# Scores of two slots in one TensorE burst, and PSUM banks shared to make room for it

## The chip, the cores and the metric

The kernel runs on one core of a Trainium2 chip. The time is that of the whole kernel on the device, in microseconds (us): inputs come from HBM, the result goes back to HBM. The engines of the core are TensorE (PE: matrix products, results go to PSUM, which has eight banks of 512 floats per partition), VectorE (DVE), ScalarE (ACT), GpSimd (POOL) and SyncE (SP, which here only issues DMAs).

## The reference

Attention with a threshold, then a two-layer network with a gated activation:

```python
def _attn_ref(q, k, v, tau):                    # 8 batches, 8 heads, 576 tokens, 64 per head
    scale = 1.0 / np.sqrt(q.shape[-1])
    scores = scale * np.matmul(q, k.transpose(0, 1, 3, 2))
    thresh = np.max(scores, axis=-1, keepdims=True) - tau
    scores = np.where(scores >= thresh, scores, -1000000000.0)
    scores = scores - np.max(scores, axis=-1, keepdims=True)
    attn = np.exp(scores)
    attn = attn / (np.sum(attn, axis=-1, keepdims=True) + 1e-09)
    return np.matmul(attn, v)

def _moe_ref(x, w_in, w_out):                   # 4608 tokens, 512 -> 2048 -> 512
    h = x @ w_in
    relu6 = np.clip(h + 3.0, 0.0, 6.0)
    g = h * relu6 / 6.0
    return g @ w_out
```

Inputs and the result are float32. Between the two parts, the heads of a token are put side by side.

## The kernel before

Four heads of a batch are a "quad", two heads a "pair": 16 quads. A quad is cut into nine "slots": slots 0 to 3 and 4 to 7 are four blocks of 128 queries of each pair, and slot 8 holds the 64 queries that are left of both pairs (576 = 4 x 128 + 64). One slot is 128 query rows of two heads, `a` = 0 and 1, which stand on the two halves of TensorE's rows. There are 144 slots, `n` = 0 to 143, in one loop, in which every engine's work stands in the order of the program.

The parts that matter here (cuts are marked):

```python
    ps_s = ctx.enter_context(tc.psum_pool(name="ps_s", bufs=2))   # scores: 2 x 2 banks
    ps_h = ctx.enter_context(tc.psum_pool(name="ps_h", bufs=1))   # projection: 2 banks
    ps_o = ctx.enter_context(tc.psum_pool(name="ps_o", bufs=1))   # output tile: 1 bank
    ps_m = ctx.enter_context(tc.psum_pool(name="ps_m", bufs=1))   # small products: 1 bank
    # ... cut
    def scores(quad, slot):
        tiles = [ps_s.tile([P, 2, 512], F32, tag="s", name="s") for _ in range(2)]
        for hf in range(2):                       # two halves of 288 keys
            if slot < 8:
                pair, t = 2 * quad + slot // 4, slot % 4
                for a in range(2):
                    nc.tensor.matmul(tiles[a][:, hf, 0:HALF], qT_of(pair)[a * 64:(a + 1) * 64, t * P:(t + 1) * P],
                                     keys(pair, a, hf), start=True, stop=True)
            # ... cut: slot 8, two pairs of 64 queries each
        return tiles

    def sm_max(sl):                               # scores out of PSUM, with the maximum of each row
        # ... cut
        for i, ps in enumerate(sl.tiles):
            nc.vector.tensor_scalar(out=sl.s[:, i, :].rearrange("p (a b) -> p a b", a=2), in0=ps[:, :, 0:HALF],
                                    scalar1=1.0, scalar2=None, op0=Alu.mult, op1=Alu.max,
                                    accum_out=sl.m[:, i:i + 1])
        nc.gpsimd.tensor_scalar(out=sl.bias[:], in0=sl.m[:], scalar1=-scale, scalar2=tau, op0=Alu.mult, op1=Alu.add)

    def mm1(item, pool=None):                     # projection: 256 or 320 tokens x 256 hidden units
        b, ni, c0, w = item
        hps = (pool or ps_h).tile([P, 2, 512], F32, tag="s" if pool else "h", name="h")
        for n in range(2):
            for ki in range(KI):
                nc.tensor.matmul(hps[:, n, 0:w], w_in_sb[:, ki, (ni + n) * P:(ni + n + 1) * P],
                                 xT[b][:, ki, c0:c0 + w], start=(ki == 0), stop=(ki == KI - 1))
        return hps[:, :, 0:w]
    # ... cut: mm1_relu on ScalarE or VectorE, mm1_gate on VectorE (into gbuf),
    #          mm2_part: 4 of the 16 matmuls of an output tile, mm2_out: the tile out of PSUM

    for n, sl in enumerate(queue):
        # ... cut
        if prev is not None:
            for i in range(2):
                sm_exp(prev, i)                   # ScalarE
        if n + 1 < len(queue):
            sm_max(queue[n + 1])                  # VectorE

        if slot != 8 and todo1:
            item, then = todo1.pop(0)
            h = mm1(item)
            r = mm1_relu(h, on_act=(slot in ((0, 1, 3, 4, 5) if quad >= 2 * NB else (0, 2, 3, 4))))
            mm1_gate(item, h, r)
            todo2.extend(then)
        # ... cut: transposes on TensorE in the first slots
        if prev is not None:
            sm_recip(prev)                        # VectorE
        pieces = 0 if slot == 3 else 1            # output pieces: one per slot, two in slot 0 or 1
        # ... cut: mm2_part for each piece
        for i in range(2):
            sm_mask(sl, i)                        # ScalarE
        if n == 1 or slot == 0 and quad > 0:
            evict = transpose_q(2 * quad + 1)     # on VectorE from batch 2 on
        elif n == 2 or slot == 1:
            evict = transpose_k(2 * quad + 1)
        elif slot == 3 and quad > 0:
            av_main(2 * quad - 1)                 # attention times v, and its copy out by VectorE
        elif slot == 4 and quad > 0:
            av_rest(quad - 1)
        # ... cut: slots 4, 5 and 6 transpose for the next quad, slot 8: av_main(2 * quad)
        if n + 2 < len(queue):
            queue[n + 2].tiles = scores(queue[n + 2].quad, queue[n + 2].slot)
        if prev is not None:
            sm_norm(prev)                         # GpSimd, then a transposing DMA
```

After the loop stand the rest of the projections and output tiles, which take turns in three PSUM buffers.

Of the kernel before, what the change touches and what calls it, by code (L numbers as in the profile page):

```python
# [16 lines left out]
HALF = 288  # L17
# [4 lines left out]
def kernel(  # L22
# [21 lines left out]
    N2 = 28  # L44
    scale = 1.0 / math.sqrt(D)
# [15 lines left out]
    ps_s = ctx.enter_context(tc.psum_pool(name="ps_s", bufs=2))  # L61
    ps_h = ctx.enter_context(tc.psum_pool(name="ps_h", bufs=1))
    ps_o = ctx.enter_context(tc.psum_pool(name="ps_o", bufs=1))
    ps_m = ctx.enter_context(tc.psum_pool(name="ps_m", bufs=1))

    ctx.enter_context(tc.manual_schedule())

# [5 lines left out]
    xT = {}  # L73
    loads = []
# [103 lines left out]
    def warm_up(count):  # L178
        warm = ps_h.tile([P, 2, 512], F32, tag="h", name="warm")
        for _ in range(count):  # L180
            nc.tensor.transpose(warm[:, 0, 0:P], identf[:], identf[:])
# [26 lines left out]
    def bank(name):  # L208
        nonlocal turn
        turn += 1  # L210
        if now < N2 and turn % 2:
            return ps_o.tile([P, 512], F32, tag="o", name=name)
        return ps_m.tile([P, 512], F32, tag="m", name=name)
# [12 lines left out]
    def main_pe(src, pair):  # L226
        ps = bank("tp")
        n = pair % 2
        for t in range(4):
            nc.tensor.transpose(ps[:, t * P:(t + 1) * P], src[:, t, 2 * n:2 * n + 2, :], identf[:])  # L230
        return ps

    def transpose_q(pair):
        nq = nat[pair // 2][0]
        if by_pe(pair):
            ps = main_pe(nq[:, 0:1024].rearrange("p (t h d) -> p t h d", h=4, t=4), pair)
            return lambda: nc.vector.tensor_copy(out=qT_of(pair)[:, 0:512], in_=ps[:])
        n = pair % 2
        nc.vector.transpose(out=qT_of(pair), in_=nq[:, n * S:(n + 1) * S])

    def transpose_k(pair):
# [5 lines left out]
        ps = main_pe(nat[pair // 2][1], pair)  # L247
        return lambda: copy_out(kT_of(pair)[:, 64:576], ps[:])

    def transpose_rest(quad, of_k=True, of_q=True):  # L250
        ps = bank("tr")
        nq, _, kr = nat[quad]
        of_q = of_q and by_pe(2 * quad)
        if of_k:
            nc.tensor.transpose(ps[:, 0:P], kr[:], identf[:])
        if of_q:
            nc.tensor.transpose(ps[:, P:2 * P], nq[:, 1024:1152], identf[:])

        def evict():
            qT, kT = qkT[quad]  # L260
            both = ps[:].rearrange("p (w n t) -> p w n t", n=2, t=64)
# [7 lines left out]
    def keys(pair, a, hf):  # L269
        kT = kT_of(pair)  # L270
        c0 = 64 * (1 - a) + hf * HALF
        return kT[a * 64:(a + 1) * 64, c0:c0 + HALF]


    def scores(quad, slot):
        tiles = [ps_s.tile([P, 2, 512], F32, tag="s", name="s") for _ in range(2)]
        for hf in range(2):
            if slot < 8:
                pair, t = 2 * quad + slot // 4, slot % 4
                for a in range(2):  # L280
                    nc.tensor.matmul(tiles[a][:, hf, 0:HALF], qT_of(pair)[a * 64:(a + 1) * 64, t * P:(t + 1) * P],  # L281
                                     keys(pair, a, hf), start=True, stop=True)
            else:
                for n in range(2):
                    for a in range(2):
                        pair = 2 * quad + n
                        nc.tensor.matmul(tiles[a][n * 64:(n + 1) * 64, hf, 0:HALF],  # L287
                                         qT_of(pair)[a * 64:(a + 1) * 64, 512:S], keys(pair, a, hf),
                                         start=True, stop=True)
        return tiles  # L290
# [4 lines left out]
    def sm_max(sl):  # L295
# [5 lines left out]
        for i, ps in enumerate(sl.tiles):  # L301
            nc.vector.tensor_scalar(out=sl.s[:, i, :].rearrange("p (a b) -> p a b", a=2), in0=ps[:, :, 0:HALF],  # L302
# [30 lines left out]
    def pe_transpose(sl):  # L333
        ps = ps_h.tile([P, 2, 1024], BF16, tag="h", name="pt")
        ps = ps[:].rearrange("p a b -> p (a b)")[:, 0:2 * S].rearrange("p (c t) -> p c t", t=P)
        pn = sl.pn[:].rearrange("p a b -> p (a b)")
        for c in range(9):
            nc.tensor.transpose(ps[:, c, :], pn[:, c * P:(c + 1) * P], identb[:])
        return lambda: nc.vector.tensor_copy(out=sl.dst, in_=ps)


    def av(ps, pair, pT, cols):
        b, hp = divmod(pair, NPAIR)
        vm, vr = vsb[b]
        for c in range(4):
            for a in range(2):
                nc.tensor.matmul(ps[a * 64:(a + 1) * 64, :], vm[:, 2 * hp + a, c * D:(c + 1) * D],  # L347
                                 pT[:, 5 * a + c, cols], start=(c == 0), stop=False)
        for a in range(2):
            nc.tensor.matmul(ps[a * 64:(a + 1) * 64, :], vr[:, a, hp, :], pT[:, 4, cols], start=False, stop=True)  # L350

    def av_main(pair):
        b, hp = divmod(pair, NPAIR)
        if hp == 0:
            xT[b] = x_pool.tile([P, KI, S], BF16, tag="xT", name="xT")
        ps = bank("av")
        av(ps[:], pair, pts[pair], slice(0, 512))
        o0 = 64 if b % 2 else 0
        nc.vector.tensor_copy(out=xT[b][:, hp, o0:o0 + 512], in_=ps[:])  # L359

    def av_rest(quad):
        b, g = divmod(quad, 2)
        ps = bank("ar")
        for n in range(2):
            av(ps[:, n * 64:(n + 1) * 64], 2 * quad + n, ptr[quad], slice(n * 64, (n + 1) * 64))
        o0 = 0 if b % 2 else 512
        nc.vector.tensor_copy(out=xT[b][:, 2 * g:2 * g + 2, o0:o0 + 64],
                              in_=ps[:, 0:P].rearrange("p (a b) -> p a b", a=2))
# [273 lines left out]
```

## Time and profile before

| | |
|---|---|
| time, median of 3 runs | 546.87 us (545.75 to 548.74) |
| span of the profiled execution | 543.9 us |
| PE busy | 524.2 us, 96% |
| ACT busy | 459.9 us, 85% |
| DVE busy | 432.6 us, 80% |
| POOL busy | 278.3 us, 51% |
| granted TensorE clock | 0.998 |
| last scores of the loop begin, end of the span | 482.1, 543.9 us |

A profile line of a group reads: line of the kernel, engine, operation, what it writes and reads, shape, count, then busy time and mean ns of one, then the engine's idle time just before and what ended it. A timeline line reads: start and duration in us, engine, line, operation, tiles, form, count. A list of waits gives us in total, times, longest. "PEld" is TensorE's loading of weights; `x8` for one slot's scores means four float32 products of two passes each.

### The profile page before, as it was taken

What the parts mean: (1) busy time and instruction counts of PE and PEld (TensorE: products, weight loads), DVE (VectorE), ACT (ScalarE), POOL (GpSimd) and SP (SyncE); (2) the same over time, 40 slices, a digit from 0 to 9 for tenths busy, and PEclk for the clock granted to TensorE, in tenths of its full rate; (3) what the DMA queues carried; (4) which work ended last, traced back from release to release, by engine and by line L of the source; (5) the groups of instructions that cost most, each with busy time, mean ns of one, the idle gap of its engine ahead of it and who ended that gap; (6) DMA issues with size and microseconds to landing.
All of it is one profiled execution on the core that took longest, in us unless ns stands there. A gap on an engine that the chain in (4) does not pass through costs nothing.

```text
span 543.9 us, 11450 instructions
## 1 busy us (share of the span) xinstructions
PE 524.2 (96%) x3801; PEld 300.9 (55%) x3801; DVE 432.6 (80%) x1059; ACT 459.9 (85%) x985; POOL 278.3 (51%) x502
## 2 busy tenths in 40 slices
PE   8999899999999999899999999999999999999997
PEld 6665565545545555555555555545555555554663
DVE  3789888888978788888989788888989788974540
ACT  3999989978989899897989899997989899993440
POOL 1787879555455445654456445654456444451000
PEclk9999999999999999999999999999999999999999
DMA  5899999969989898998689798998689886544102
GB/s 125 128 156 158 143 148 179 181 83 177 158 159 182 136 167 149 155 176 146 112 152 201 130 168 132 183 159 145 133 149 202 134 163 111 111 102 104 40 17 81
DMA packets 308139, 76.63 MB, mean 141 GB/s; under 512 B 291056, under 2 KB 303600, under 8 KB 308080
## 3 DMA queue, kind: packets, MB, share of 16 engines
q1 hardware_dynamic: 289472, 66.59, 69.6%
q0 software_dynamic: 17408, 8.92, 14.3%
q8 instruction: 30, 0.49, 0.4%
q10 hardware_dynamic: 1200, 0.39, 0.3%
q14 instruction: 29, 0.24, 0.1%
HBM read 36.70 MB, written 9.44 MB: 85 GB/s over the span
## 4 chain that ended last, share of the span: by engine, by line
PE 60%; ACT 11%; DVE 11%; issue 3%; DMA 2%; POOL 2%; DVEq 0%; POOLq 0%
PE h L377 18%; PE o L406 17%; PE s L281 16%; ACT s L309 4%; PE av L347 4%; ACT s L314 4%; DVE s L302 4%; ACT r L386 2%; DVE g L394 2%; DMA pR<-pn 2%; DVE r L388 2%; PE s L287 1%; POOL pn L322 1%; DVE osb L414 1%; PE av L350 1%
## 5 line engine op out<-in xcount | busy, mean ns | idle before, releaser
L322 POOL TENSOR_SCALAR pn<-s,rinv 128x576 bf16<-128x576 f32 x288 | 211.7, 748 | 122.9 <-issue 49.7
L302 DVE TENSOR_SCALAR_CACHE_REDUCE s<-s 128x576 f32<-128x576 f32 x288 | 205.8, 752 | 32.5 <-PE s L281 20.9
L309 ACT ACTIVATE s<-s,bias 128x576 f32<-128x576 f32 x288 | 205.9, 763 | 6.3 <-POOL bias L305 5.9
L314 ACT ACTIVATE s<-s 128x576 f32<-128x576 f32 x288 | 192.5, 670 | 0.3
L281 PE MATMUL s<-kT,qT 64*128 64x288 f32 x1024 | 169.8, 429 | 2.1 <-DVE s L302 1.3
L377 PE MATMUL h<-xT,w_in_sb 128*128 128x320 bf16 (+1 forms) x1024 | 144.8, 287 | 4.2 <-DVE g L394 3.1
L406 PE MATMUL o<-w_out_sb,g 128*128 128x512 bf16 x576 | 140.7, 379 | 2.8 <-DVE osb L414 2.8
L281 PEld LDWEIGHTS s<-kT,qT 64*128 64x128 f32 x1024 | 96.2, 186 | 60.2 <-DVE s L302 24.8
L377 PEld LDWEIGHTS <-w_in_sb 128*128 128x128 bf16 x1024 | 91.4, 98 | 68.2 <-issue 33.1
L394 DVE SCALAR_TENSOR_TENSOR g<-r,h 128x512 bf16<-128x512 f32 (+1 forms) x128 | 96.4, 755 | 30.2 <-ACT r L386 28.7
L386 ACT ACTIVATE r<-h,three 128x640 f32<-128x640 f32 (+1 forms) x85 | 62.8, 740 | 42.5 <-PE h L377 41.0
L406 PEld LDWEIGHTS <-g 128*128 128x128 bf16 x576 | 55.6, 98 | 56.4 <-issue 7.7
L305 POOL TENSOR_SCALAR bias<-m 128x2 f32<-128x2 f32 x144 | 27.3, 190 | 89.2 <-DVE s L302 71.4
L314 ACT ACTIVATION_READ_ACCUMULATOR s<-s 128x1 f32 x288 | 54.4, 189 | 0.0
L414 DVE TENSOR_SCALAR osb<-o 128x512 f32<-128x512 f32 x31 | 21.0, 676 | 22.1 <-PE o L406 21.9
L347 PE MATMUL av<-pT,vm 128*64 128x512 bf16 x256 | 33.7, 385 | 1.7 <-DMA pT<-pn 1.3
L388 DVE TENSOR_SCALAR r<-h 128x512 f32<-128x512 f32 (+1 forms) x43 | 32.4, 753 | 0.0
L347 PEld LDWEIGHTS <-vm 128*64 128x64 bf16 x512 | 17.7, 110 | 25.2 <-issue 15.8
L359 DVE CAST xT<-av 128x512 bf16<-128x512 f32 x32 | 21.9, 684 | 10.9 <-PE av L350 10.8
L317 DVE RECIPROCAL rinv<-rsum 128x2 f32<-128x2 f32 x144 | 22.9, 159 | 2.3 <-ACT s L314 2.3
L302 DVE DVE_READ_ACCUMULATOR s<-s 128x1 f32 x288 | 24.0, 83 | 0.0
L287 PE MATMUL s<-kT,qT 64*64 64x288 f32 x256 | 21.5, 416 | 0.6 <-DVE s L302 0.6
(57 smaller groups left out, 226.2 us busy)
## 6 DMA issues: line engine op xcount, KB each, us to landing
out_dram<-osb SPq DMA_DIRECT2D x31, 256.0 KB, 2.6
nq<-in_q_dram SPq DMA_DIRECT2D x96, 72.0 KB, 2.9
km<-in_k_dram SPq DMA_DIRECT2D x96, 64.0 KB, 2.6
vm<-in_v_dram POOLq DMA_DIRECT2D x16, 256.0 KB, 6.1
km<-in_k_dram SPq DMA_DIRECT2D x16, 128.0 KB, 3.9
w_in_sb<-in_moe_w_in_dram POOLq DMA_DIRECT2D x16, 128.0 KB, 4.7
w_out_sb<-in_moe_w_out_dram POOLq DMA_DIRECT2D x16, 128.0 KB, 4.5
pT<-pn SPq DMA_TRANSPOSE x117, 3.4
```

What stands on the lines that cost most here:

```text
L281: nc.tensor.matmul(tiles[a][:, hf, 0:HALF], qT_of(pair)[a * 64:(a + 1) * 64, t * P:(t + 1) * P], keys(pair, a, hf), start=True, stop=True)
L302: nc.vector.tensor_scalar(out=sl.s[:, i, :].rearrange("p (a b) -> p a b", a=2), in0=ps[:, :, 0:HALF], scalar1=1.0, scalar2=None, op0=Alu.m ...
L305: nc.gpsimd.tensor_scalar(out=sl.bias[:], in0=sl.m[:], scalar1=-scale, scalar2=tau, op0=Alu.mult, op1=Alu.add)
L309: nc.scalar.activation(out=s, in_=s, func=Act.Prelu, bias=sl.bias[:, i:i + 1], scale=scale, alpha=REJECT)
L314: nc.scalar.activation(out=s, in_=s, func=Act.Exp, accum_out=sl.rsum[:, i:i + 1])
L322: nc.gpsimd.tensor_scalar(out=pn[:, i, :], in0=sl.s[:, i, :], scalar1=sl.rinv[:, i:i + 1], scalar2=1.0, op0=Alu.mult, op1=Alu.mult)
L347: nc.tensor.matmul(ps[a * 64:(a + 1) * 64, :], vm[:, 2 * hp + a, c * D:(c + 1) * D], pT[:, 5 * a + c, cols], start=(c == 0), stop=False)
L377: nc.tensor.matmul(hps[:, n, 0:w], w_in_sb[:, ki, (ni + n) * P:(ni + n + 1) * P], xT[b][:, ki, c0:c0 + w], start=(ki == 0), stop=(ki == KI ...
L386: nc.scalar.activation(out=r, in_=hps, func=Act.Relu, bias=three[:])
L388: nc.vector.tensor_scalar(out=r, in0=hps, scalar1=3.0, scalar2=0.0, op0=Alu.add, op1=Alu.max)
L394: nc.vector.scalar_tensor_tensor(out=gbuf[:, ni:ni + 2, c0:c0 + w], in0=r, scalar=6.0, in1=hps, op0=Alu.min, op1=Alu.mult)
L406: nc.tensor.matmul(o_ps[0], gbuf[:, ni, mt * P:(mt + 1) * P], w_out_sb[:, ni, :], start=(ni == 0), stop=(ni == NI - 1))
```

## The change

From slot 23 on the scores of two slots are computed in one burst, at every odd slot `n`: those of `n + 3`, then those of `n + 2`. The purpose is that TensorE goes half as often into the products of half its rows and back. Two slots of scores need six PSUM banks (576 columns of two slots, two heads). The other two are for the projection (`HB`) and the output tile (`OB`). Three things follow from that:

- The small products (transposes on TensorE, attention times v) use banks 2 and 5 of the score banks, alternately. Scores of odd slots lie partly in these two banks, so they come after the small product's copy, which is put after the next maximum in odd slots ("waiting").
- A projection has one bank: 512 instead of up to 640 elements. So 512 tokens of each batch are projected in blocks of 256, and the 64 odd tokens of two batches are put together: they are the weights (128 tokens), `w_in` streams, and the gated result, which has tokens on its rows, is transposed by a DMA into `gbuf`. There are 144 projections instead of 128, in every slot.
- Output pieces come two at a time in even slots; which relus are ScalarE's, and in which slots q and k are transposed, is set anew.

The core of the diff (cuts are marked):

```diff
-    ps_s = ctx.enter_context(tc.psum_pool(name="ps_s", bufs=2))
-    ps_h = ctx.enter_context(tc.psum_pool(name="ps_h", bufs=1))
-    ps_o = ctx.enter_context(tc.psum_pool(name="ps_o", bufs=1))
-    ps_m = ctx.enter_context(tc.psum_pool(name="ps_m", bufs=1))
+    go_pool = ctx.enter_context(tc.tile_pool(name="go", bufs=1))
+    ps_pool = ctx.enter_context(tc.psum_pool(name="ps", bufs=1))
+    ps = ps_pool.tile([P, 8, 512], F32, name="ps")
+    ps_flat = ps[:].rearrange("p b c -> p (b c)")
...
-    def bank(name):
+    def bank():
         nonlocal turn
         turn += 1
-        if now < N2 and turn % 2:
-            return ps_o.tile([P, 512], F32, tag="o", name=name)
-        return ps_m.tile([P, 512], F32, tag="m", name=name)
+        return ps[:, (2, 5)[turn % 2], :]
...
+    def first(n):
+        return n > N1 + 2 and n % 2
+
+    def score_col(n, a):
+        return (704 if first(n) else 128) + (0 if a else 1536)
+
+    def scores(n):
+        quad, slot = divmod(n, NSLOT)
+        w0 = 320 if first(n) else 384
+        for k0, w in ((0, w0), (w0, S - w0)):
...
-    def mm1(item, pool=None):
-        b, ni, c0, w = item
-        hps = (pool or ps_h).tile([P, 2, 512], F32, tag="s" if pool else "h", name="h")
-        for n in range(2):
+    def mm1(item, hb=HB):
+        b, ni, c0 = item
+        if c0 is None:
             for ki in range(KI):
-                nc.tensor.matmul(hps[:, n, 0:w], w_in_sb[:, ki, (ni + n) * P:(ni + n + 1) * P],
-                                 xT[b][:, ki, c0:c0 + w], start=(ki == 0), stop=(ki == KI - 1))
-        return hps[:, :, 0:w]
+                nc.tensor.matmul(ps[:, hb, :], xR[b // 2][:, ki, :], w_in_sb[:, ki, ni * P:ni * P + 512],
+                                 start=(ki == 0), stop=(ki == KI - 1))
+        else:
+            for n in range(2):
+                for ki in range(KI):
+                    nc.tensor.matmul(ps[:, hb, n * 256:(n + 1) * 256], w_in_sb[:, ki, (ni + n) * P:(ni + n + 1) * P],
+                                     xT[b][:, ki, c0:c0 + 256], start=(ki == 0), stop=(ki == KI - 1))
+        return ps[:, hb, :]
...
+        if c0 is None and ni % 8 == 4:
+            nc.sync.dma_start_transpose(out=gbuf[:, ni - 4:ni + 4, 512:512 + P], in_=odd[0][:])
...
         if n + 1 < len(queue):
             sm_max(queue[n + 1])
-
-        if slot != 8 and todo1:
+        for copy in waiting:
+            copy()
+        waiting = []
+
+        if todo1:
             item, then = todo1.pop(0)
             h = mm1(item)
-            r = mm1_relu(h, on_act=(slot in ((0, 1, 3, 4, 5) if quad >= 2 * NB else (0, 2, 3, 4))))
+            r = mm1_relu(h, on_act=(slot in ((0, 2, 4, 8) if quad < 2 * NB else (0, 1, 3, 4) if quad % 2 else (0, 4, 5, 8))))
             mm1_gate(item, h, r)
...
-        for _ in range(pieces):
-            if todo2:
-                bb, mt, part = todo2.pop(0)
-                mm2_part(bb, mt, part)
+        for _ in range(2 if n % 2 == 0 and todo2 else 0):
+            bb, mt, part = todo2.pop(0)
+            mm2_part(bb, mt, part)
...
-        if n == 1 or slot == 0 and quad > 0:
-            evict = transpose_q(2 * quad + 1)
-        elif n == 2 or slot == 1:
-            evict = transpose_k(2 * quad + 1)
...
+        t0 = 3 if quad % 2 and quad > 1 else 4
+        t1 = -1 if quad % 2 == 0 and quad > 2 else 0 if quad else 1
+        if slot == t1 or slot == 8 and quad % 2 and 1 < quad < NQUAD - 1:
+            evict.append(transpose_q(2 * (quad + slot // 8) + 1))
+        if slot == t1 + 1:
+            evict.append(transpose_k(2 * quad + 1))
...
+        if n < N1 or n % 2:
+            for copy in waiting:
+                copy()
+            waiting = []
...
-        if n + 2 < len(queue):
-            queue[n + 2].tiles = scores(queue[n + 2].quad, queue[n + 2].slot)
+        if n <= N1:
+            scores(n + 2)
+        elif n % 2:
+            for m in (n + 3, n + 2):
+                if m < len(queue):
+                    scores(m)
```

`N1` is 22. Up to slot 22 one slot is scored at a time, as before, and the q and k of the first two batches are transposed on TensorE. After the loop the projections take turns in four banks and the output tiles in two.

## The prediction

> **What bounds the kernel now.** I read the page first (busy shares), then the share of each engine in one steady stretch, the groups of instructions, and last the timeline of two engines. The stretch is 247.7 to 370.2 us: 36 slots, four quads, from one start of slot 72's masks to that of slot 108's.
>
> ```profile
> PE 524.2 (96%) x3801; PEld 300.9 (55%) x3801; DVE 432.6 (80%) x1059; ACT 459.9 (85%) x985; POOL 278.3 (51%) x502
> ...
> 247.70:370.20 122.50, 121.23 (x885) 67.33 (x884) 107.08 (x261) 112.54 (x245) 65.15 (x116) 1.00 0.91 155
> ...
> PEld s L281 <- DVE s L302: 24.8, 61, 0.9
> PEld L377 <- DVE g L394: 11.1, 19, 0.9
> ```
>
> The first line is the whole run, the second the stretch (its length, then busy us of PE, weight loads, DVE, ACT, POOL). PE is busy 99% there, ACT 92%, DVE 87%. The last two, from the list of waits, say what TensorE's weight loads lose to VectorE: little over a whole run, but these are the two places where it can wait. A busy PE is not a PE at its peak, so I take its costs from starts, not from durations:
>
> ```profile
> 306.62 1.24 PE L281 MATMUL s<-kT,qT 64*128 64x288 f32 x8
> 307.80 1.05 PE L377 MATMUL h<-xT,w_in_sb 128*128 128x256 bf16 x8
> 308.68 1.89 PE L406 MATMUL o<-w_out_sb,g 128*128 128x512 bf16 x8
> 310.50 1.24 PE L281 MATMUL s<-kT,qT 64*128 64x288 f32 x8
> 311.68 1.05 PE L377 MATMUL h<-xT,w_in_sb 128*128 128x256 bf16 x8
> 312.56 1.03 PE L406 MATMUL o<-w_out_sb,g 128*128 128x512 bf16 x4
> 313.52 1.24 PE L281 MATMUL s<-kT,qT 64*128 64x288 f32 x8
> ...
> 307.99 0.76 DVE L302 TENSOR_SCALAR_CACHE_REDUCE s<-s 128x576 f32<-128x576 f32 x1 [0.56 <-PE s L281]
> 308.67 0.75 DVE L302 TENSOR_SCALAR_CACHE_REDUCE s<-s 128x576 f32<-128x576 f32 x1
> 309.35 0.08 DVE L302 DVE_READ_ACCUMULATOR s<-s 128x1 f32 x1
> 309.60 0.69 DVE L394 SCALAR_TENSOR_TENSOR g<-r,h 128x512 bf16<-128x512 f32 x1 [0.17 <-ACT r L386]
> 310.21 0.16 DVE L317 RECIPROCAL rinv<-rsum 128x2 f32<-128x2 f32 x1
> 310.28 0.76 DVE L239 STREAM_TRANSPOSE qT<-nq 128x576 f32<-128x576 f32 x1
> ```
>
> Start to start: scores of a slot 1.17, a projection of 512 columns 0.88, one output piece (four matmuls) 0.96, two 1.82; so a piece is 0.86 and 0.10 is the step into the scores. Within a burst the pairs of score passes start 0.236 apart, after 0.34 for the first pair (single starts in the trace): 4 x 0.236 = 0.94 is work, 0.23 is entry and leaving. On VectorE: scores' start to their maximum 1.37, the two maxima 1.36, relu 0.72, gate 0.61, reciprocal 0.07; projection's start to its gate, with the relu on ScalarE, 1.80 (307.80 to 309.60).
>
> **What the skill says.** "TensorEngine Tiling", Key Properties: a change of tiling mode drains TensorE. The trace agrees: 0.10 in, 0.23 of first load and way out. "TensorE: Matmul & The Clock Gate", The mechanism: row groups of the array work at the same time. Agrees: the two heads' passes start 7 ns apart, and where one head's waits, the other goes 0.31 us ahead and ends so (burst at 316.53). "PSUM — Partial Sum Buffer", PSUM bank collisions: accesses of two engines are to be kept apart by bank; here that shows as the wait of each writer for the last reader. "Perfetto Trace Analysis", Matmuls: independent groups should rotate through banks. The change goes the other way for the projections (one bank) and for transposes and attention outputs (they borrow score banks 2 and 5); no run here shows yet what that costs.
>
> **The change part by part** (per 36 slots).
>
> Removed on PE: from 36 bursts to 18. Saved 18 x (0.23 + 0.10) = 5.9 us.
>
> Projections: a pair of batches had 32 items (16 of 512, 16 of 640 elements), now 36 of 512: 8192 columns of odd tokens either way (16 x 4 x 128 before, 16 x 512 now). PE gains nothing. Gate and relu get 4 more instructions each; 640 against 512 elements is 0.738 against 0.605 start to start, so +0.3 us of gates. The relu moves: 16 of 36 on ScalarE instead of 21 of 33 records, 20 on VectorE instead of 12: ScalarE 111.5 to about 107, VectorE (sum of start to start) 103.8 to 109.0.
>
> PE's own sum before: 32 x 1.17 + 4 x 1.13 scores, 3.5 entries, 31.5 projections, 31 output pieces, 9.6 + 1.8 attention outputs (0.89 + 0.31 and 0.44 each), 0.8 transposes = 120 of 122.5: the stretch is PE's. After: 120 - 5.9 + about 1 for the entries that attention outputs no longer share with scores = 115. If PE stayed the bound this is 7.5 us per 36 slots, x 121/36 slots = 25 us, 522 us.
>
> Added: a longer loop. Before, scores of n+2 wait for the maximum of n+1, then VectorE has gate, relu and reciprocal to do while they run: 1.37 + 1.36 + 0.14 (release) = 2.9 us a slot (0.14: 0.08 of the accumulator's read and 0.06 to the weight load), under PE's 3.0 to 3.2. After, one burst at odd n writes n+3, then n+2, and waits for the maximum of n+1; in VectorE's order the maximum of n+2 comes first, then the gate of slot n+1, then the maximum of n+3, after which the next burst may go. The gate belongs to a projection that stands behind the burst on PE. From the start of the (later head's) burst:
> - 2 slots of scores 1.17 + 0.94 = 2.11, then the projection. Relu on ScalarE: gate at 2.11 + 1.80 = 3.91; gate and reciprocal 0.68; a q or k transpose on VectorE, which stands in the same iteration in 4 of 9 pairs, 0.65; maxima 1.36; release 0.14: **6.74**.
> - Relu on VectorE (no transpose there): 2.11 + 1.05 + 0.04 + 0.72 + 0.68 + 1.36 + 0.14 = **6.10**.
> - PE alone: 0.88 + 1.72 + 0.88 + 2.11 + 0.10 = 5.69; with an attention output 1.30 more = 7.0, with both kinds 7.45.
>
> The first head's maximum frees the first head's matmul 0.68 earlier; this is already in: without it each would be some 0.4 longer.
>
> Nine pairs of slots make two quads. Greater of loop and PE: pairs (0,1), (4,5) and (1,2): 6.74 each; (6,7) and (5,6): 6.10; (2,3), (8,0), (7,8): 7.0; (3,4) of the odd quad: gate, transpose and attention output, 7.45 by PE. In two odd iterations the last matmul of the burst waits for the attention output's copy out of bank 2 or 5, behind relu, gate and transpose: about 0.45 and 0.35. Sum 20.2 + 12.2 + 21.0 + 7.45 + 0.8 = 61.7, or 123.3 per 36 slots against 122.5. So the 7.5 that PE saves turns into waiting; VectorE is the bound in half of the pairs.
>
> On top: odd tokens' projection must wait for its copy of the attention rest, which now stands behind the next maximum (about 1 us per pair of batches, three times); 64-column scores of slot 8 within a burst of 128-column ones may drain again (0.2 a quad). After the loop: 109 output pieces lie before the last scores now, 106 then: 3 x 0.86 = 2.6 us move to the tail, where PE never waits, plus 20 x 0.88 + 5 x 0.88 = 22.0 for 21.5 us of projections. The eight new transposing DMAs (after 131 of the kind) end some five items before they are needed.
>
> Sum: loop +0.8 x 3.36 = +2.7; copies and drains +1 to +6; tail +3, of which the loop gives back 0 to 2.6. About 546.9 + 3.5 = **550**.
>
> **Rivals.** (1) PE stays the bound: 522 to 530. For it: 99% busy now, and the relu's places are chosen so that VectorE's transposes and relus never meet, as if someone balanced it. Against: the loop above has 2.3 us of burst in it that VectorE can't bridge in even iterations. (2) Worse: ScalarE's relu isn't on time (its idle before the relu was 11.6 us of the stretch, so it usually is early, but it is 107 of 123 busy), or the stagger of the heads is not kept: 0.3 to 0.5 a pair, x 60 = 18 to 30 us, 565 to 575. (3) The shared banks cost nothing and transposes fit into VectorE's waits: 543.
>
> **Range and chances.** Loop sums of this kind came out 2% short for the kernel before (120 against 122.5), so I put 550 in the middle, 532 to 566 for 8 in 10. Faster by over 2% (under 536) needs the loop to be wrong by 4%: 0.2. Slower by over 2% (over 557.8) needs 2.5 us more per 36 slots: 0.3.
>
> **What would show it.** PE's busy share in the steady stretch falls from 99% to about 93%, with waits of score loads and projections for the maximum and the gate of some 7 us per 36 slots; score groups are 18, some 2.1 us each; VectorE's share rises to 90% or so; a pair of slots takes 6.1 to 7.4 us. The tail after the last scores is 3 us longer. Wrong if PE stays busy 98% or more of that stretch (idle 1.3 us of 122.5 now): then rival 1.

## The result, and the profile after

| | before | after |
|---|---|---|
| time, median | 547.67 us (545.75 to 548.8, 6 runs) | 569.04 us (568.41 to 571.29, 6 runs) |
| ratio, 95% interval | | 1.040 (1.037 to 1.043) |
| span of the profiled execution | 543.9 us | 566.6 us |
| steady stretch, slots 72 to 108 | 122.5 us | 128.7 us |
| slot 143's maximum to the end of the span | 60.4 us | 64.9 us |

The kernel became 4.0% slower; 550 with a range of 532 to 566 had been predicted. First the page of the kernel after: busy shares, the chain of work that ended last by engine, and the groups of the maximum and of the scores.

```profile
PE 532.5 (94%) x3865; PEld 321.2 (57%) x3865; DVE 444.0 (78%) x1099; ACT 450.4 (79%) x977; POOL 277.2 (49%) x502
...
PE 45%; DVE 23%; issue 7%; ACT 6%; DMA 4%; POOL 2%; SPq 2%; POOLq 0%; DVEq 0%
...
L299 DVE TENSOR_SCALAR_CACHE_REDUCE s<-ps 128x576 f32<-128x576 f32 x288 | 205.3, 749 | 47.7 <-PE ps L284 40.4
...
L284 PE MATMUL ps<-kT,qT 64*128 64x192 f32 (+7 forms) x1280 | 193.9, 422 | 8.5 <-DVE s L299 4.7
```

Of the chain of the kernel before, VectorE had 11% and TensorE 60%; now they have 23% and 45%. The path to the end runs through VectorE twice as long. The windows of the same kernel, the steady stretch and one early stretch (length, busy us of PE, weight loads, DVE, ACT, POOL; then clock, DMA share, GB/s):

```profile
248.50:377.10 128.60, 124.13 (x900) 72.73 (x900) 110.64 (x274) 108.91 (x241) 64.88 (x116) 1.00 0.89 152
155.00:190.00 35.00, 28.31 (x196) 16.03 (x197) 26.10 (x65) 27.21 (x60) 17.34 (x30) 0.90 1.10 161
```

TensorE reads 124.13 of 128.60, 96.5% busy, as if little were lost. But the work in those 36 slots, counted from starts of groups that nothing held up, is 14 bursts x 2.14 + 4 bursts with a slot 8 x 2.30 = 39.2, projections 18 x 0.88 + 18 x 0.97 = 33.3 (the dearer ones have the step into a burst behind them), output pieces 31.9, attention outputs 11.4, transposes 0.8: 116.6 us. So 12 us are waiting, 7.9 of them inside the bursts, where the busy share counts them as work (by single bursts, 5.2 for the second head's maximum and 2.7 for copies out of a shared bank). The list of waits shows where they begin (total, times, longest, whole run):

```profile
DVE s L299 <- PE ps L284: 40.4, 49, 1.7
...
PEld ps L284 <- DVE s L299: 23.1, 64, 1.1
...
PEld ps L284 <- DVE xT L354: 6.0, 12, 1.2
...
PEld L373 <- DVE xR L364: 5.2, 4, 1.6
...
PE ps L378 <- DVE g L401: 5.1, 11, 1.1
```

Both directions are there: VectorE waits for scores, and the scores' weight loads wait for VectorE's maximum and for its copies of small products (`xT`, `xR`). It is a ring of two engines. The last line is a projection that waits for the gate before it to leave the one bank. Now TensorE's timeline over two pairs of slots:

```profile
279.42 2.72 PE L284 MATMUL ps<-kT,qT 64*128 64x384 f32 x16
282.07 1.05 PE L378 MATMUL ps<-xT,w_in_sb 128*128 128x256 bf16 x8
282.96 1.89 PE L412 MATMUL ps<-w_out_sb,g 128*128 128x512 bf16 x8
284.78 1.05 PE L343 MATMUL ps<-pT,vm 128*64 128x512 bf16 x8
285.66 0.38 PE L346 MATMUL ps<-pT,vr 128*64 128x512 bf16 x2
285.98 1.05 PE L378 MATMUL ps<-xT,w_in_sb 128*128 128x256 bf16 x8
286.96 2.21 PE L284 MATMUL ps<-kT,qT 64*128 64x384 f32 x16
289.10 1.04 PE L373 MATMUL ps<-w_in_sb,xR 128*128 128x512 bf16 x4
289.97 1.89 PE L412 MATMUL ps<-w_out_sb,g 128*128 128x512 bf16 x8
291.76 1.02 PE L373 MATMUL ps<-w_in_sb,xR 128*128 128x512 bf16 x4
293.10 2.88 PE L284 MATMUL ps<-kT,qT 64*128 64x384 f32 x16 [0.32 <-DVE s L299]
295.92 1.05 PE L378 MATMUL ps<-xT,w_in_sb 128*128 128x256 bf16 x8
```

The burst at 286.96 takes 2.14 us to the next start; those at 279.42 and 293.10 take 2.65 and 2.82 for the same 16 products, with no gap in the record. What happens inside is seen in the weight loads, of the burst at 293.10 and of two others:

```profile
272.60 0.11 PEld L373 LDWEIGHTS <-xR 128*128 128x128 bf16 x2 [1.58 <-DVE xR L364]
...
293.10 0.29 PEld L284 LDWEIGHTS ps<-kT,qT 64*128 64x128 f32 x2 [0.82 <-DVE s L299]
...
293.78 1.80 PEld L284 LDWEIGHTS ps<-kT,qT 64*128 64x128 f32 x14 [0.38 <-DVE s L299]
...
301.23 1.27 PEld L284 LDWEIGHTS ps<-kT,qT 64*128 64x128 f32 x12
...
303.23 0.30 PEld L284 LDWEIGHTS ps<-kT,qT 64*128 64x128 f32 x4 [0.72 <-DVE xR L364]
```

At 293.10 one head's loads begin, the other's 0.68 later, when its maximum is done. At 303.23 the last product of both heads waits for the copy out of a shared bank (that burst takes 2.62). The first line is the odd tokens' projection, which waits 1.58 us for the same kind of copy.

### The profile page after: what moved, and what is told of

Same layout as the page of the kernel before. It is cut to its first block, busy times and chain, and to the rows that moved or that the text cites. A ratio compares the mean times of both kernels' runs of the same rounds, so it can differ in the third digit from the quotient of the medians.

```text
span 566.6 us, 11592 instructions
## 1 busy us (share of the span) xinstructions
PE 532.5 (94%) x3865; PEld 321.2 (57%) x3865; DVE 444.0 (78%) x1099; ACT 450.4 (79%) x977; POOL 277.2 (49%) x502
## 4 chain that ended last, share of the span: by engine, by line
PE 45%; DVE 23%; issue 7%; ACT 6%; DMA 4%; POOL 2%; SPq 2%; POOLq 0%; DVEq 0%
PE ps L284 17%; PE ps L378 12%; DVE s L299 10%; PE ps L412 9%; PE ps L343 3%; ACT r L386 3%; DVE r L388 3%; DVE g L401 3%; POOL pn L319 2%; DMA pT<-pn 2%; ACT s L306 2%; DVE qT L238 2%; ACT s L311 1%; DVE kT L244 1%; DVE rinv L314 1%
## 5 line engine op out<-in xcount | busy, mean ns | idle before, releaser
L299 DVE TENSOR_SCALAR_CACHE_REDUCE s<-ps 128x576 f32<-128x576 f32 x288 | 205.3, 749 | 47.7 <-PE ps L284 40.4
L284 PE MATMUL ps<-kT,qT 64*128 64x192 f32 (+7 forms) x1280 | 193.9, 422 | 8.5 <-DVE s L299 4.7
L284 PEld LDWEIGHTS ps<-kT,qT 64*128 64x128 f32 (+1 forms) x1280 | 116.4, 176 | 75.1 <-DVE s L299 23.1
L378 PE MATMUL ps<-xT,w_in_sb 128*128 128x256 bf16 x1024 | 131.3, 274 | 6.7 <-DVE g L401 5.1
L412 PE MATMUL ps<-w_out_sb,g 128*128 128x512 bf16 x576 | 133.5, 379 | 0.0
L401 DVE SCALAR_TENSOR_TENSOR g<-r,ps 128x512 bf16<-128x512 f32 x128 | 87.9, 687 | 26.1 <-ACT r L386 24.0
L386 ACT ACTIVATE r<-ps,three 128x512 f32<-128x512 f32 x77 | 52.7, 685 | 59.1 <-PE ps L378 48.5
L311 ACT ACTIVATION_READ_ACCUMULATOR s<-s 128x1 f32 x288 | 54.5, 189 | 0.0
L388 DVE TENSOR_SCALAR r<-ps 128x512 f32<-128x512 f32 x67 | 45.9, 685 | 0.6 <-PE ps L378 0.6
L343 PE MATMUL ps<-pT,vm 128*64 128x512 bf16 x256 | 34.6, 393 | 3.6 <-DMA pT<-pn 3.6
L299 DVE DVE_READ_ACCUMULATOR s<-ps 128x1 f32 x288 | 23.8, 83 | 0.0
L314 DVE RECIPROCAL rinv<-rsum 128x2 f32<-128x2 f32 x144 | 22.7, 158 | 0.0
```

The lines of the kernel that those rows point to most:

```text
L284: nc.tensor.matmul(ps_flat[rows, c0:c0 + w], qT_of(pair)[a * 64:(a + 1) * 64, q0:q0 + rows.stop - rows.start], kT_of(pair)[a * 64:(a + 1) ...
L299: nc.vector.tensor_scalar(out=sl.s[:, i, :], in0=ps_flat[:, c0:c0 + S], scalar1=1.0, scalar2=None, op0=Alu.mult, op1=Alu.max, accum_out=sl ...
L311: nc.scalar.activation(out=s, in_=s, func=Act.Exp, accum_out=sl.rsum[:, i:i + 1])
L314: nc.vector.reciprocal(out=sl.rinv[:], in_=sl.rsum[:])
L343: nc.tensor.matmul(pb[a * 64:(a + 1) * 64, :], vm[:, 2 * hp + a, c * D:(c + 1) * D], pT[:, 5 * a + c, cols], start=(c == 0), stop=False)
L378: nc.tensor.matmul(ps[:, hb, n * 256:(n + 1) * 256], w_in_sb[:, ki, (ni + n) * P:(ni + n + 1) * P], xT[b][:, ki, c0:c0 + 256], start=(ki = ...
```

## The experiments

Four explanations were set against each other. **A**: the loop of burst, first maximum, gate, second maximum, next burst, in VectorE's order. **B**: the small products in score banks 2 and 5. **C**: the rest of the change (projections of one bank, odd tokens, pieces in pairs, a lower clock in places). **D**: VectorE is short of time as a whole. "Slower" and "faster" below are differences of medians against the 569.04 us of the kernel after; they are good to some 2 us, since the runs stand on several chips. Ratios are against the kernel before on the same chip.

**e1: one slot per burst, all else of the change kept.**

```diff
     def first(n):
-        return n > N1 + 2 and n % 2
+        return False
...
-        if n <= N1:
+        if n + 2 < len(queue):
             scores(n + 2)
-        elif n % 2:
-            for m in (n + 3, n + 2):
-                if m < len(queue):
-                    scores(m)
```

> The changed kernel with one slot per burst (scores of n + 2 at every n, always in the same four banks); one-bank projections, odd tokens as weights, pieces in pairs and the places of relus and transposes stay. Theory A (the burst of two slots makes a loop through VectorE: burst, maximum, gate, maximum, burst): the loop is gone, TensorE pays 5.9 us more per 36 slots and is the bound again: 548 to 556 us. Theory B (small products in the score banks cost it): banks 2 and 5 no longer hold scores, so it also recovers, to the same 548 to 556; A and B are told apart by the other runs. Theory C (one-bank projections, the odd tokens' path, pieces in pairs and the lower clock they bring cost it): stays within 1% of 569.

Measured: 583.45 us, ratio 1.067 (1.064 to 1.070): slower by 14 us, which none had expected. TensorE's timeline of this kernel:

```profile
279.94 1.98 PE L284 MATMUL ps<-kT,qT 64*128 64x384 f32 x8
282.54 1.03 PE L378 MATMUL ps<-xT,w_in_sb 128*128 128x256 bf16 x8 [0.62 <-DVE g L401]
283.41 1.89 PE L412 MATMUL ps<-w_out_sb,g 128*128 128x512 bf16 x8
...
286.43 1.24 PE L284 MATMUL ps<-kT,qT 64*128 64x384 f32 x8
287.61 1.05 PE L378 MATMUL ps<-xT,w_in_sb 128*128 128x256 bf16 x8
```

With both pieces in the even slot, the odd slot has one projection, 0.9 us, between two bursts; VectorE can't be ready by then, and every second burst takes 2.60 to the next start instead of 1.18. The experiment undid the burst but not what had been fitted to it; e5 mends that.

**e2: the order within the burst turned round.** The slot that lies partly in banks 2 and 5 is then scored first.

```diff
-            for m in (n + 3, n + 2):
+            for m in (n + 2, n + 3):
```

> The changed kernel with the two slots of a burst in the other order: n + 2 first, then n + 3. Theory A: only the second half of the burst then waits for the maximum of n + 1, and the maximum of n + 2 can begin about 1 us earlier, so the loop is 1 us shorter in the 5 of 9 pairs without an attention output: 555 to 562 us. Theory B: the first half now waits for the copy of the small product, the whole burst is late in odd slots with small products: 572 to 580. Theory C: 569.

Measured: 586.51 us, ratio 1.074 (1.069 to 1.080), slower by 17. TensorE's timeline of this kernel, one burst:

```profile
309.35 0.81 PE L284 MATMUL ps<-kT,qT 64*128 64x320 f32 x4
311.35 1.67 PE L284 MATMUL ps<-kT,qT 64*128 64x256 f32 x12 [1.19 <-DVE xR L364]
312.95 1.05 PE L378 MATMUL ps<-xT,w_in_sb 128*128 128x256 bf16 x8
```

The burst stops for 1.19 us after a quarter, for a small product's copy. Over the run the score loads wait 15.4 us for `xT` and 10.6 for `xR`, against 6.0 and 2.9 in the kernel after. Pairs without an attention output don't get shorter (6.30 for 6.28, 6.15 for 6.14), so A's expectation of a gain failed; the time also lies above B's range of 572 to 580. The order that the change chose is the right one, and copies out of the shared banks are on the path.

**e3: all attention outputs in even slots**, so that their copy is made in the next, odd slot, well before the burst at its end, and not in the slot of the burst itself.

```diff
-        if slot == 3 and quad > 0:
+        even = n > N1 + 2
+        if slot == (2 if even and quad % 2 == 0 else 3) and quad > 0:
             waiting.append(av_main(2 * quad - 1))
-        elif slot == 4 and quad > 0:
+        elif slot == (5 if even and quad % 2 else 4) and quad > 0:
...
+        if even and slot == 0 and quad % 2 == 0:
+            waiting.append(av_main(2 * quad - 2))
...
-        if slot == 8:
+        if slot == 8 and not (even and quad % 2 and quad < NQUAD - 1):
             waiting.append(av_main(2 * quad))
```

> The changed kernel with the attention outputs of odd slots moved to even slots (slot 3 to 2, 4 to 5, 8 to the next 0), so that no burst stands right behind a small product that shares its banks. Theory B: 555 to 562. Theory A: the waits for the maxima stay; only the late copies in two of nine pairs (0.8 us of 18 slots, 5 us in all) go: 562 to 566. Theory C: 569.

Measured: 556.71 us, ratio 1.018 (1.015 to 1.021): faster by 12.3, within what B expected. From the list of waits of this kernel:

```profile
DVE s L299 <- PE ps L284: 25.5, 36, 2.1
...
PEld ps L284 <- DVE s L299: 19.0, 59, 1.1
```

The first was 40.4: with the last product on time, VectorE gets its scores on time.

**e4: q and k transposed on VectorE in odd slots only.** Short form of the edit, from quad 3 on:

```diff
-        if slot == t1 or slot == 8 and quad % 2 and 1 < quad < NQUAD - 1:
-            evict.append(transpose_q(2 * (quad + slot // 8) + 1))
-        if slot == t1 + 1:
-            evict.append(transpose_k(2 * quad + 1))
+        # odd quad:  slot 2 q, 4 k, 5 rest, 6 q, 8 k; slot 0 k of its own second pair
+        # even quad: slot 3 q, 5 k, 6 rest, 7 q
```

> The changed kernel with all q and k transposes on VectorE put into odd slots (from quad 4 on), behind the maximum that frees the burst. Theory A: 0.65 us leave the loop in 4 of 9 pairs, of which one is bound by TensorE: up to 12 us off, 557 to 563, less where the odd slots' own VectorE work gets too long. Theories B and C: 569, or more, as copies of small products in odd slots come later.

Measured: 560.74 us, ratio 1.026 (1.021 to 1.030): faster by 8.3, A's expectation.

**e5: e1 with one output piece per slot**, so that the burst and what belongs to it are both undone.

```diff
-        for _ in range(2 if n % 2 == 0 and todo2 else 0):
+        for _ in range(1 if todo2 else 0):
```

> As the kernel with one slot per burst (583.5), but with one output piece in every slot instead of two in even slots. In e1 every second burst took 2.60 us: in odd slots TensorE had only 0.9 us of other work between two bursts, and the second waited for VectorE's maxima. Theory A (undoing the burst undoes the loss, e1 was hampered by the pieces in pairs): 545 to 556. Theory C (the one-bank projections and odd tokens cost it): 565 or more.

Measured: 554.97 us, ratio 1.018 (1.013 to 1.022). The burst, together with the pieces in pairs that belong to it, therefore costs 569.04 - 554.97 = 14.1 us (some 12 by the ratios), and the rest of the change 554.97 - 546.44 (before, same chip) = 8.5. In these 8.5 the relus and transposes still stand where they were put for the bursts. In e1 the place of the pieces alone made 28.5.

**e6 and e7: a VectorE operation more, whose result nothing uses**, at the end of each even slot (e6) or odd slot (e7).

```diff
+    junk = singles.tile([P, 384], F32)
...
+        if n > N1 + 2 and n % 2 == 0:        # e7: == 1
+            nc.vector.tensor_scalar(out=junk[:], in0=junk[:], scalar1=1.0, scalar2=None, op0=Alu.mult)
```

> The changed kernel with one more VectorE operation (a product in place of 128x384 floats, some 0.3 to 0.5 us, its result unused) at the end of each even slot from 26 on: between the gate and the next maximum, inside the loop of theory A. Theory A: the whole length of it, 59 times, in pairs not bound by TensorE: +12 to +25 us over 569. Theory D (VectorE is short of time as a whole, whatever the order): the same as e7.

> The same operation at the end of each odd slot, beside the burst, where VectorE waits for the scores. Theory A: little of it, 0 to +8 us over 569. Theory D: as much as e6.

Measured: e6 585.82 us, ratio 1.073 (1.067 to 1.078); e7 571.85 us, ratio 1.047 (1.042 to 1.052). The group of that operation in e6, and then in e7 (count, busy us, mean ns of one):

```profile
L558 DVE TENSOR_SCALAR junk<-junk 128x384 f32<-128x384 f32 x59 | 27.3, 463 | 0.0
```

```profile
L558 DVE TENSOR_SCALAR junk<-junk 128x384 f32<-128x384 f32 x60 | 28.6, 477 | 0.0
```

The same 28 us of VectorE's time cost 16.8 us in even slots, where they stand between a burst and the maximum that releases the next, and 2.8 in odd slots. D is out: VectorE has time; A's order decides what a piece of its work costs.

**e8: e3 and e4 together.**

> The changed kernel with the attention outputs in even slots and the transposes in odd slots (e3 and e4 together, 12.3 and 8.3 us off alone). Theory A with B: the two are different waits and add up, 546 to 551. If both only relieved the same wait: 555.

Measured: 552.71 us, ratio 1.013 (1.009 to 1.017): faster by 16.3, of 12.3 + 8.3 = 20.6 had they simply added, and so between the two expectations. The steady stretch takes 122.3, as long as before.

**e9: e8, with the odd tokens' projections after the first eight ordinary ones** instead of first, so that they don't wait for their copy.

```diff
-        for c0, mts in (((0, (4, 5, 6)), (256, (7, 8))) if b % 2 else ((0, (0, 1)), (256, (2, 3)))):
+        for c0, mts in (((0, (5, 6)), (256, (4, 7, 8))) if b % 2 else ((0, (0, 1)), (256, (2, 3)))):
...
-            items[0:0] = [((b, 4 * f, None), ()) for f in range(2)]
-            items[5:5] = [((b, 4 * f, None), ()) for f in range(2, 4)]
+            items[8:8] = [((b, 4 * f, None), ()) for f in range(2)]
+            items[13:13] = [((b, 4 * f, None), ()) for f in range(2, 4)]
```

> e8 (attention outputs in even slots, transposes in odd slots; 552.7) with the odd tokens' four projections of a batch pair behind its first eight ordinary ones, and the output tile of the odd tokens with the last two tiles. Theory C (what the rest of the change costs): the odd tokens' projection no longer waits 0.7 us for its copy, and output pieces no longer run out around slots 46 to 50, where TensorE's clock fell: slots 50 to 56 take 21 instead of 25 us, 546 to 549. If the clock falls elsewhere instead: 552.

Measured: 549.44 us, ratio 1.0035 (1.0013 to 1.0056). The steady stretch got shorter (121.6 for 122.3); slots 50 to 56 did not fall to 21 us as expected, they take 23.5.

**e10: e9, with the relu of every even slot on ScalarE and of every odd slot on VectorE; e11: the kernel after with that edit alone.**

```diff
-            r = mm1_relu(h, on_act=(slot in ((0, 2, 4, 8) if quad < 2 * NB else (0, 1, 3, 4) if quad % 2 else (0, 4, 5, 8))))
+            r = mm1_relu(h, on_act=(n % 2 == 0))
```

> As e9, and the relu of every even slot on ScalarE, of every odd slot on VectorE (18 and 18 of 36, before 16 and 20). Theory A: the even slots' 0.72 us of relu leave the loop in the pairs without a VectorE transpose, for a relu on ScalarE that ends 0.7 us after the projection: 0.3 to 0.5 us in 3 of 9 pairs, 4 to 8 us less than e9. Theory D (VectorE short as a whole): 3 us less (2 of 20 relus move in 36 slots). If ScalarE's relu comes late in even slots: no gain.

> The changed kernel with only the relu moved as in e10; transposes stay, half of them in even slots where the relu is ScalarE's already. Theory A: 4 to 8 us off 569, less what odd slots lose where relu, gate and transpose now stand before a small product's copy: 562 to 569. Theory D: 566.

Measured: e10 546.70 us, ratio 0.999 (0.996 to 1.002); e11 563.63 us, ratio 1.031 (1.024 to 1.037), faster by 5.4. e10's gain on e9, 2.7 us, is less than A expected (4 to 8) and no more than D did (3), and e11's lies near D's number too, so these two times alone don't tell A from D; e6 and e7 do. What e10 shows in single pairs of slots is told in the next section.

**e12: e10, with the bursts from slot 35 on instead of 23.** Until then one slot per burst and one piece per slot; the new places of small products and relus also begin there, and in even slots of the bursts a second piece is left out where an output tile ends (both left out below).

```diff
+    NBU = 34
...
-        return n > N1 + 2 and n % 2
+        return n > NBU + 2 and n % 2
...
-        for _ in range(2 if n % 2 == 0 and todo2 else 0):
+        for _ in range(min(len(todo2), 1) if n <= NBU else 0 if n % 2 or not todo2 else 2):
...
-        if n < N1 or n % 2:
+        if n < NBU or n % 2:
...
-        if n <= N1:
+        if n <= NBU:
             scores(n + 2)
```

> e10 (546.7) with the bursts of two slots from slot 35 on instead of 23, and one output piece in every slot until then: up to there q and k are transposed on TensorE, through banks 2 and 5, and the stretch from slot 23 to 36 took 43.6 us against 41.4 in the kernel before. Theories A and B: that stretch falls to about 41.5, 543 to 545. If that stretch is bound by the DMAs whatever the order: 546 to 547.

Measured in 11 runs: 542.06 us (540.46 to 545.13), ratio 0.9926 (0.9895 to 0.9956). This beats both kernels, the one before by 0.7%. Its steady stretch, in the windows' columns as above:

```profile
239.60:359.60 120.00, 119.39 (x901) 71.96 (x901) 109.90 (x272) 110.48 (x243) 64.88 (x116) 1.00 0.95 163
```

VectorE does the same 110 us of work as in the kernel after, in 120.0 instead of 128.6 us.

All by stages, in us between the starts of the first maximum of those slots:

| slots | before | after | e5 | e6 | e7 | e3 | e4 | e8 | e9 | e10 | e12 |
|---|---|---|---|---|---|---|---|---|---|---|---|
| 0 to 23 | 65.9 | 65.5 | 65.5 | 65.9 | 65.9 | 65.5 | 65.5 | 65.5 | 65.5 | 65.5 | 65.5 |
| 23 to 36 | 41.4 | 44.9 | 42.1 | 45.7 | 45.0 | 44.0 | 44.9 | 44.1 | 44.1 | 43.6 | 42.0 |
| 36 to 56 | 71.5 | 73.6 | 73.6 | 73.8 | 76.2 | 71.0 | 71.1 | 72.6 | 72.3 | 69.6 | 68.9 |
| 56 to 72 | 54.6 | 55.6 | 54.7 | 58.1 | 55.9 | 55.3 | 54.9 | 54.6 | 54.5 | 53.8 | 53.8 |
| 72 to 108 | 122.5 | 128.7 | 124.1 | 134.6 | 129.1 | 124.5 | 126.0 | 122.3 | 121.6 | 120.0 | 120.0 |
| 108 to 143 | 118.4 | 124.6 | 120.5 | 129.3 | 124.9 | 120.6 | 121.5 | 118.8 | 118.1 | 117.7 | 117.0 |
| 143 to end | 60.4 | 64.9 | 64.9 | 64.9 | 65.0 | 64.8 | 64.9 | 64.9 | 64.6 | 64.9 | 64.6 |

## Why the prediction was wrong

The direction and the mechanism were right: TensorE's saving turns into waiting for VectorE's order. The size was not: +3.5 us against a span longer by 22.7. By the table, 13.4 of these come from slots 56 to 143, 4.5 from the tail, 3.4 from slots 23 to 36, 2.0 from slots 36 to 56; the part before slot 23 gives 0.6 back. In the steady stretch, what failed is one term of the sum, the pair of slots whose relu is on VectorE; late copies took more than was put for them, too.

**Removed on PE: nearly right.** A burst was to take 2.11 us; unhindered it takes 2.14, and 2.30 with a slot 8. TensorE's own sum was to be 115 and is 116.6. The Trainium skill's "TensorEngine Tiling (Array Packing)", Key Properties, says that a change of tiling mode drains TensorE, and this trace agrees: two bursts of one slot take 2 x 1.17 and two entries of 0.10, one of two slots 2.14 and one entry.

**The loop with its relu on VectorE: the step that failed.** The prediction's sums run from the start of the later head of one burst to the start of the later head of the next. Read so from the weight loads (slots 72 to 89), and for comparison from the first head, nine pairs of slots take:

| pair | (0,1) | (2,3) | (4,5) | (6,7) | (8,0) | (1,2) | (3,4) | (5,6) | (7,8) | sum |
|---|---|---|---|---|---|---|---|---|---|---|
| predicted | 7.09 | 7.00 | 6.74 | 6.10 | 7.00 | 6.74 | 7.45 | 6.55 | 7.00 | 61.7 |
| measured, later heads | 7.70 | 6.92 | 7.83 | 6.79 | 7.02 | 6.83 | 7.45 | 7.13 | 7.49 | 65.2 |
| measured, first heads | 7.02 | 7.60 | 7.83 | 6.28 | 7.54 | 6.14 | 8.14 | 6.60 | 8.01 | 65.2 |

(The late copies, 0.45 and 0.35, are put with the pair whose burst they hold up.) By first heads the pairs with an attention output seem too long, but only because a wait of the second head, 0.5 or 0.7 us, is then counted with the pair after the loop that causes it. By later heads the rule "greater of loop and PE" holds: (1,2), a loop with a transpose, takes 6.83 for 6.74, and TensorE's pairs (2,3), (8,0) and (3,4) take 6.92, 7.02 and 7.45 for 7.00, 7.00 and 7.45. The edits agree. e6 makes (1,2) longer, 7.42, and leaves TensorE's pairs as they were (6.92, 7.03, 7.46, and 7.50 for (7,8)); e4, which takes the transpose out of it, makes it 6.21.

What is wrong is a term: 6.10 for a pair whose relu is on VectorE. It lets the relu start as soon as the projection is done, 1.05 + 0.04 = 1.09 us after the projection's start. In the trace of (5,6) it starts after 1.56 (303.86 to 305.42), behind both maxima of the burst that has just ended (lines of TensorE's and of VectorE's timeline):

```profile
303.86 1.05 PE L378 MATMUL ps<-xT,w_in_sb 128*128 128x256 bf16 x8
...
304.06 0.76 DVE L299 TENSOR_SCALAR_CACHE_REDUCE s<-ps 128x576 f32<-128x576 f32 x1 [0.88 <-PE ps L284]
...
304.74 0.75 DVE L299 TENSOR_SCALAR_CACHE_REDUCE s<-ps 128x576 f32<-128x576 f32 x1
...
305.42 0.69 DVE L388 TENSOR_SCALAR r<-ps 128x512 f32<-128x512 f32 x1
306.14 0.69 DVE L401 SCALAR_TENSOR_TENSOR g<-r,ps 128x512 bf16<-128x512 f32 x1
306.74 0.16 DVE L314 RECIPROCAL rinv<-rsum 128x2 f32<-128x2 f32 x1
306.82 0.73 DVE L299 TENSOR_SCALAR_CACHE_REDUCE s<-ps 128x576 f32<-128x576 f32 x1
...
307.48 0.75 DVE L299 TENSOR_SCALAR_CACHE_REDUCE s<-ps 128x576 f32<-128x576 f32 x1
...
310.87 0.76 DVE L299 TENSOR_SCALAR_CACHE_REDUCE s<-ps 128x576 f32<-128x576 f32 x1 [0.63 <-PE ps L284]
...
313.69 1.03 PE L378 MATMUL ps<-xT,w_in_sb 128*128 128x256 bf16 x8 [0.26 <-DVE g L401]
```

VectorE does seven things in a row, from 304.06 on, before both heads of the next burst (which starts at 307.84) are free. The prediction took the first head's lead over the second as given ("without it each would be some 0.4 longer"). Where the lead is there, as in (2,3) with 0.68, the relu starts 1.15 after the projection (260.53 to 261.68). In the bursts ahead of (6,7) and (5,6) both heads start together, the maxima and the relu come later, and the two pairs are 0.69 and 0.58 too long; 0.16 of the 0.69 is a burst with a slot 8. In (7,8) the late relu makes the gate late, and the next projection, which has one bank, waits for it and starts 2.15 us after the two output pieces instead of 1.73 (last line). e10 against e9 tests it, since only the places of the relus differ. The sums give 6.10 for the relu on VectorE and 6.74 - 0.65 = 6.09 for ScalarE, so (6,7) should not change. It falls from 6.79 to 6.32, in both of the stretch's two sets of nine pairs. e11 against the kernel after does the same (6.79 to 6.31).

Over the whole stretch the pairs take 128.7 for 123.3. Of these 5.3 us too many, the relu's place makes about 2.7 (0.5 in (6,7) and in (5,6), 0.3 in (7,8), twice); 0.6 is the copy at the first (0,1), which holds its burst up for 1.00 instead of 0.35, as the copy of an output tile (0.60) stands ahead of it in VectorE's order; 1.1 is the first (4,5), where the odd tokens' projection waits 1.26 for its copy and a third late copy, not foreseen, takes 0.32; 0.8 are bursts with a slot 8. The odd tokens and slot 8 the prediction had counted apart. e3, which takes the late copies away, makes the stretch 4.2 us shorter; the copies themselves held bursts up for 2.7, where 1.6 had been put. The rest of e3's gain comes with attention outputs now standing in other pairs.

**The early slots.** The +0.8 per 36 slots of the steady stretch was applied to slots 23 to 36 as well. That stage got 3.4 us longer; with the burst undone (e5: 42.1) or begun later (e12: 42.0) most of it goes away. Why the burst costs more there than later was not tested.

**Copies and drains, +1 to +6.** The odd tokens' projections wait for their copy 5.2 us in four weight loads, 1.3 each, near the 1 us predicted. Moving them (e9 against e8) is worth 3 us by the medians, 5 by the ratios. The four bursts with a slot 8 in a stretch cost 0.16 more each, near the 0.2 said.

**Tail, +3: measured +4.5.** After the last scores there are now 16 pieces instead of 13 (13.92 for 11.33 us, the predicted 2.6), and the projections take 23.1 us for 22.1 (20 in 17.68 and five in 5.43, for 16 in 16.23 and five in 5.87). Of this 1.0, where 0.5 was said, 0.89 is a wait that was not foreseen, for a transposing DMA behind the five (it is in the 5.43):

```profile
512.16 1.05 PE L343 MATMUL ps<-pT,vm 128*64 128x512 bf16 x8 [0.89 <-DMA pT<-pn]
```

The other 0.9 stands ahead of the five: from the last burst to there TensorE now has two projections instead of one and takes 4.99 us for 4.12. No experiment changed the tail; e12 still pays 4.2.

**Not foreseen: slots 50 to 56.** The kernel after was 3.1 us ahead in slots 36 to 50 and lost 5.1 in the next six. In the window 155 to 190 us above the granted clock is 0.90. One line of TensorE's timeline there, and a window inside it (columns as above):

```profile
167.63 1.92 PE L343 MATMUL ps<-pT,vm 128*64 128x512 bf16 x8 [2.72 <-DMA pT<-pn]
...
166.90:173.70 6.80, 6.07 (x42) 3.20 (x44) 3.38 (x9) 3.26 (x8) 2.37 (x5) 0.50 1.33 224
```

The output pieces had run out, so nothing filled the wait for the transposing DMA. During this wait the granted clock fell to 0.50 and stayed there for 6.8 us; the products in that time took 1.92 us instead of 1.05. An estimate: at half the clock for 6.8 us, at most 3.4 of the 5.1 us are the clock's. It is not all of it: e6 keeps a clock of 1.00 there and still takes 23.7 us for these six slots. The kernel before, with 20.7, has no such fall of the clock in its loop. The net +2.0 of slots 36 to 56 is not the burst's, since e5 has the same 73.6 there (54.2 and 19.4, for 47.8 and 25.8). In e10 and e12 slots 50 to 56 still take 23.5 and 24.7. Why the DMA lands late there was not tried, and whether the wait brought the clock down is not shown.

**The signs.** 18 score groups came as said, VectorE's share is 86% (90 said), pairs take 6.8 to 7.8 from later head to later head (6.1 to 7.4 said). "TensorE's busy share falls to 93%" was a bad sign: it is 96.5% with 12 us of waits. The Trainium skill's "Perfetto Trace Analysis", Identifying the Most-Contended Engine, warns that matmul busy time does not tell how close TensorE is to its limit, because matmuls are pipelined; this stretch agrees that the share misleads, here because blocks of matmuls hide waits. Of the rivals, 1 (522 to 530) and 3 (543) fell. 2 (565 to 575) has the time, and one of its two reasons in part: the stagger of the heads is indeed not kept, but only in the bursts ahead of some pairs. That ScalarE's relu is late was not seen: VectorE's gates wait 30.1 us for it over the whole run, and did 28.7 before.

So the burst is not worthless. e10 still has bursts from slot 23 and its steady stretch is 120.0 against 122.5: 2.5 of the 7.5 us that TensorE's sum had promised. Whether e10's other edits would help as much with one slot per burst was not tried, so e12's gain over the kernel before is not shown to be the burst's.

## What to carry to other kernels

When work on one engine is grouped to save its entries, write out the other engine's whole order between two groups, with the operations that the finished group itself sets off: here two maxima came before the relu and made pairs half a microsecond longer. A piece of work costs much before the operation that releases the next group and little after it (here 16.8 against 2.8 us for the same operation). Whatever borrows a bank from the group has to be copied out a whole step before the group needs it. Compare a prediction with the trace between the very points that its sums run between (here later head to later head, not first to first), and undo a grouping together with whatever was fitted to it.

## What the runs showed of the hardware

The two halves of TensorE's rows run apart within one burst: at 293.10 the second head's loads begin 0.68 us after the first's, and the burst is recorded as one busy block of 2.88 us. A wait of one half thus shows in little or no idle time, only in a longer block (2.14 to 2.82 from start to start). In the like burst at 257.71 the first head's products of 320 columns begin at 1.12 us, before the second head's of 192 columns (1.43), which stand ahead of them in the program. The lead is no gain for what TensorE does next: the projection starts 2.14 us after the later head (293.78 to 295.92), as in a burst without a wait.

The granted clock can halve in the middle of a busy kernel: it was 0.50 for 6.8 us, from 166.9 on, in the kernel after, and eight products took 1.92 us instead of 1.05. It fell during a wait of 2.72 us on TensorE; a wait of 2.44 us in e6 (172.29) came with no such fall.
